# Keys, query weights and output weights of a decode kernel loaded in 4 KB runs, raw keys through the value ring

## The chip, the cores and the metric

One core of one Trainium2 chip. The metric is the device time of one launch in microseconds (us). A time "of n runs" is a median; all runs of this study were in the fast state, with a granted clock of 1.0. In the profiles PE is the matmul engine and PEld its weight loads, DVE the vector engine, ACT the scalar engine, POOL GpSimd, and SPq the queue of SyncE, which issues all loads.

## The reference, cut to what matters

Two rounds of grouped-query attention for one new token, each followed by a small FFN. Both attention rounds read the same key and value cache, 8 sequences x 8 key heads x 8192 positions x 128, in bf16: 134 MB of keys and 134 MB of values.

```python
def _A_ref(x, k_cache, v_cache, wq, wo):          # x [8,1,512], wq [512,4096], wo [4096,512]
    q = (x @ wq).reshape(B, Sq, 32, 128).transpose(0, 2, 1, 3)
    scores = einsum("bhqd,bhkd->bhqk", q, k) * 128 ** -0.5      # four query heads share a key head
    p = softmax(scores); o = einsum("bhqk,bhkd->bhqd", p, v)
    return o.transpose(0, 2, 1, 3).reshape(B, Sq, 4096) @ wo
x = x + _A_ref(layernorm(x), ...);  x = x + _B_ref(layernorm(x), w1, w2)     # _B_ref: w2 @ silu(w1 @ x)
x = x + _A_ref(layernorm(x), ...);  x = x + _B_ref(layernorm(x), w1, w2)
```

The second round's queries depend on the first round's result, so a sequence's values are read twice. Its keys (17 MB) are read once and kept turned on the chip for the second round.

## The kernel before

A "unit" is one round of attention (layer 0 or 1) for one sequence b and key head g. A pass interleaves layer 1 of sequence b with layer 0 of sequence b+1. All loads come in pieces of 512 KB ("granules", 4 KB on each of 128 partitions), in one fixed order on one queue; a load waits for its place, and those behind it wait too. Values, wq and wo go into a ring of 10 places, keys into 33 places of their own, where DVE turns them (32x32 transposes of 32-bit words) into the place before.

```python
N_GRAN = 10; N_PIECE = 33; N_DEF = 2              # ring places, key pieces, units held over a boundary

def load_v(b, g, P):                              # 4 KB contiguous per partition
    return load_gran(f"v{b}.{g}.{P}", v_src(b, g)[P], 1)

def load_k(b, g):
    src = A_k_cache[b, g].rearrange("(p c4 cg) d -> p c4 (cg d)", p=128, c4=4)
    for q in range(4):                            # four runs of 1 KB per partition
        m = 4 * (G * b + g) + q                   # may start when the piece lying there was scored by layer 1
        n = plan.load(f"k{b}.{g}.{q}", 0.5, None, None, [scored.get(m - N_PIECE + 1)])
        ... dma(sp, piece(m + 1)..., src[:, :, 4 * DH * q:4 * DH * (q + 1)], ...)

def load_wq(g): return load_gran(f"wq{g}", wq_v[:, :, R * DH * g:R * DH * (g + 1)], KT)   # 1 KB runs
def load_wo(g): return load_gran(f"wo{g}", wo_v[:, R * g:R * (g + 1), :], R)              # 1 KB runs

def turns(b, g):                                  # two transposes of 512 words per piece
    ... tn.append(plan.add(f"t{b}.{g}.{q}", "DVE", 1.25, turn, count[0] + 0.5, [kn] + tn[-1:]))
# scores of piece q wait for turn q; then maximum (DVE), all-reduce (POOL), subtraction (DVE),
# exponent (ACT), sum (DVE), all-reduce (POOL), reciprocal (DVE)
```

A small planner simulates engines and loads at build time with these durations. The order in which it finds things done becomes the static instruction order of each engine; the semaphores come from the data alone. Between two passes lies the "boundary": layer 0 of the last unit, output projection, FFN, norm, the first query of layer 1, its scores and exponents. Two units of the pass before are held back so that their values can be loaded meanwhile.

## Time and profile before

| | before |
|---|---|
| time, median of 3 | 1325.4 us |
| bytes moved by the load queue | 481.9 MB |
| mean rate over the span | 366 GB/s |
| packets of 1 KB / 4 KB | 206608 / 65536 |
| DVE, PE busy | 54%, 49% |

The prediction below shows the rows for the queue and the rates. These two rows of the page belong beside them: the busy time of each engine, and the shares of the chain that ended last.

```profile
PE 652.5 (49%) x20384; PEld 598.1 (45%) x20384; DVE 721.2 (54%) x1456; ACT 52.2 (4%) x138; POOL 116.3 (9%) x291
DMA 50%; DVE 16%; issue 14%; SPq 14%; PE 4%; POOL 2%; POOLq 0%; ACT 0%; DVEq 0%
```

No engine is near full, and half the last chain is transfers. Three stretches of the windows view, a pass, the first boundary and a later one (columns: start and end, length, busy time of five engines with instruction counts, granted clock, DMA share, GB/s):

```profile
160.00:290.00 130.00, 63.32 (x1950) 57.63 (x1951) 76.05 (x146) 4.99 (x13) 10.98 (x27) 1.00 1.06 380
132.50:160.00 27.50, 14.53 (x468) 13.56 (x468) 13.40 (x32) 1.33 (x4) 3.57 (x8) 1.00 0.68 240
610.00:635.00 25.00, 13.62 (x439) 12.68 (x436) 13.22 (x34) 1.15 (x3) 2.98 (x7) 1.00 0.95 348
```

Within a pass the queue is full at the rate of its mix of 1 and 4 KB; at the boundaries it is not full.

### The profile page before, as it was taken

Reading aid. Unit: us, or ns where it says so; the run is one execution under the profiler, and the core shown is the slowest. Engines: PE = TensorE matmul, PEld = TensorE weight load, DVE = VectorE, ACT = ScalarE, POOL = GpSimd, SP = SyncE. Lnnn points to the kernel's source line nnn. Section 1 sums busy time; section 2 is a strip of 40 time slices with the busy share of each in tenths; the row PEclk is TensorE's granted clock in tenths of the full one; section 3 lists DMA queues with packets and bytes.
Section 4 is the critical chain, followed back from the end, with each engine's and each line's share of the span. In section 5 each row is a group of like instructions: output and inputs, shape, how many; then the busy total and the mean of one; then the engine's idle time right before and its main releaser. Section 6 shows DMA issues by size and latency. Waiting matters only on the chain.

```text
span 1325.2 us, 45128 instructions
## 1 busy us (share of the span) xinstructions
PE 652.5 (49%) x20384; PEld 598.1 (45%) x20384; DVE 721.2 (54%) x1456; ACT 52.2 (4%) x138; POOL 116.3 (9%) x291
## 2 busy tenths in 40 slices
PE   2324544555544554445554454554554555444555
PEld 2323544444544544445444454444543454444554
DVE  7644465735568265673466645484465736567221
ACT  0000000000000000000000000000000000000000
POOL 1000100100000010010000000000000100001000
DMA  9999799999999999999999999999999999999995
GB/s 327 373 369 381 264 380 379 371 391 357 380 377 373 357 383 379 375 377 359 379 385 369 389 350 379 377 373 388 330 385 376 369 378 371 378 378 376 387 367 198
DMA packets 287392, 484.78 MB, mean 366 GB/s; under 512 B 14544, under 2 KB 221152, under 8 KB 287200
## 3 DMA queue, kind: packets, MB, share of 16 engines
q1 hardware_dynamic: 287200, 481.90, 101.3%
q8 instruction: 160, 2.62, 0.8%
q14 instruction: 32, 0.26, 0.1%
HBM read 481.83 MB, written 0.01 MB: 364 GB/s over the span
## 4 chain that ended last, share of the span: by engine, by line
DMA 50%; DVE 16%; issue 14%; SPq 14%; PE 4%; POOL 2%; POOLq 0%; ACT 0%; DVEq 0%
DMA kts<-in_A_k_cache_dram 30%; DVE kts L609 14%; DMA ring<-in_A_v_cache_dram 14%; SPq L310 14%; DMA ring<-in_A_wq_dram 6%; PE ot L733 1%; POOL small L695 1%; PE misc L571 1%; POOL small L676 1%; DVE sc L681 1%; PE misc L479 0%; PE sc L659 0%; DVE small L671 0%; PE yt L761 0%; DVE small L690 0%
## 5 line engine op out<-in xcount | busy, mean ns | idle before, releaser
L609 DVE STREAM_TRANSPOSE kts<-kts 128x512 uint32<-128x512 uint32 x512 | 511.2, 1073 | 71.7 <-DMA kts<-in_A_k_cache_dram 63.4
L659 PE MATMUL sc<-bd,kts 128*128 128x16 bf16 x8192 | 279.5, 175 | 285.0 <-DVE kts L609 214.1
L659 PEld LDWEIGHTS sc<-bd,kts 128*128 128x128 bf16 x8192 | 248.5, 104 | 303.4 <-DVE kts L609 226.8
L733 PE MATMUL ot<-p,ring 128*128 128x4 bf16 x8192 | 284.2, 167 | 171.2 <-DMA ring<-in_A_v_cache_dram 156.0
L733 PEld LDWEIGHTS ot<-p,ring 128*128 128x128 bf16 x8192 | 252.3, 104 | 191.6 <-DMA ring<-in_A_v_cache_dram 175.1
L671 DVE TENSOR_REDUCE small<-sc 128x4 f32<-128x256 f32 x128 | 51.9, 405 | 121.9 <-PE sc L659 121.9
L676 POOL PARTITION_ALL_REDUCE small<-small x128 | 48.2, 376 | 713.2 <-DVE small L671 686.4
L686 ACT ACTIVATE p<-sc 128x256 bf16<-128x256 f32 x128 | 49.2, 384 | 1145.9 <-DVE sc L681 1145.9
L571 PE MATMUL misc<-xn,ring 128*128 128x1 bf16 (+1 forms) x1152 | 42.1, 166 | 92.5 <-DMA ring<-in_A_wq_dram 86.4
L695 POOL PARTITION_ALL_REDUCE small<-small x128 | 55.1, 430 | 345.0 <-DVE small L690 303.3
L571 PEld LDWEIGHTS misc<-xn,ring 128*128 128x128 bf16 x1152 | 36.5, 105 | 97.5 <-DMA ring<-in_A_wq_dram 92.3
L745 DVE TENSOR_TENSOR attna<-ot,small 128x4 bf16<-128x4 f32 x64 | 10.0, 157 | 123.8 <-PE ot L733 123.8
L681 DVE TENSOR_TENSOR sc<-sc,small 128x256 f32<-128x256 f32 x128 | 56.6, 443 | 36.5 <-POOL small L676 36.5
L690 DVE TENSOR_REDUCE small<-p 128x4 f32<-128x256 bf16 x128 | 50.8, 397 | 31.0 <-ACT p L686 31.0
L761 PE MATMUL yt<-attna,ring 128*128 128x1 bf16 x1024 | 36.4, 165 | 34.0 <-DVE attna L745 33.9
L643 DVE TENSOR_TENSOR bd<-qx,mask 128x64 bf16<-128x64 f32 x128 | 27.9, 218 | 45.6 <-PE qx L635 45.1
L761 PEld LDWEIGHTS yt<-attna,ring 128*128 128x128 bf16 x1024 | 32.8, 104 | 37.3 <-issue 37.3
L635 PE MATMUL qx<-qab,sel 128*128 128x4 bf16 x256 | 16.5, 169 | 50.2 <-DVE bd L643 39.3
L699 DVE RECIPROCAL small<-small 128x4 f32<-128x4 f32 x128 | 21.4, 167 | 30.9 <-POOL small L695 30.5
L635 PEld LDWEIGHTS qx<-qab,sel 128*128 128x128 bf16 x256 | 11.9, 106 | 52.7 <-DVE bd L643 41.1
L579 DVE CAST qtb<-misc 128x4 bf16<-128x4 f32 x64 | 9.7, 152 | 38.5 <-PE misc L571 38.3
L635 PE MATMUL qx<-qtb,sel 128*128 128x4 bf16 x256 | 16.7, 170 | 15.8 <-DVE qtb L579 15.8
(55 smaller groups left out, 147.4 us busy)
## 6 DMA issues: line engine op xcount, KB each, us to landing
ring<-in_A_v_cache_dram SPq DMA_DIRECT2D x512, 512.0 KB, 10.3
kts<-in_A_k_cache_dram SPq DMA_DIRECT2D x256, 512.0 KB, 10.2
ring<-in_A_wq_dram SPq DMA_DIRECT2D x72, 512.0 KB, 11.0
ring<-in_A_wo_dram SPq DMA_DIRECT2D x64, 512.0 KB, 10.6
kts<-in_A_wo_dram SPq DMA_DIRECT2D x2, 2048.0 KB, 14.6
w<-in_B_w_dram SPq DMA_DIRECT2D x2, 1792.0 KB, 13.7
ring<-in_A_x_dram SPq DMA_DIRECT2D x1, 8.0 KB
out_dram<-ring SPq DMA_DIRECT2D x1, 8.0 KB
```

Source lines behind the costliest of these rows:

```text
L310: eng.dma_start(out_ap, in_ap).then_inc(counter.sem, 16)
L571: steps.append(lambda h=h, kt=kt: pe.matmul(qp[:, h * nb:(h + 1) * nb], wt[:, kt, h * DH:(h + 1) * DH], xn[:, b0:b0 + nb, kt], start=(kt = ...
L609: op(dve, lambda f=f: dve.transpose(new[:, f], raw[:, f]), reads=[res("kp", (m + 1) % N_PIECE)], writes=[res("kp", m % N_PIECE)], add=(f > 0))
L659: steps.append(lambda cg=cg, fe=fe: pe.matmul(sc[:, 16 * cg:16 * cg + 16], kv[:, cg % 4, fe // 2, fe % 2], bd[:, 16 * fe:16 * fe + 16], st ...
L671: op(dve, lambda: dve.tensor_reduce(mxp[sm], sv.rearrange("p (k h) -> p h k", h=R), AX.X, ALU.max), reads=[res(*scr)], writes=[res("mxp", ...
L676: op(pool, lambda: pool.partition_all_reduce(mxa[sm], mxp[sm], 128, bass.bass_isa.ReduceOp.max), reads=[res("mxp", sm)], writes=[res("mxa" ...
L681: op(dve, lambda: dve.tensor_tensor(v, v, mxa[sm].unsqueeze(1).to_broadcast([128, NCH, R]), ALU.subtract), reads=[res("mxa", sm)], writes= ...
L686: op(act, lambda: act.activation(pt[:, :], sv, ACT.Exp, scale=SM_SCALE), reads=[res(*scr)], writes=[res("p", sm)])
L690: op(dve, lambda: dve.tensor_reduce(ssm[sm], pt[:, :].rearrange("p (k h) -> p h k", h=R), AX.X, ALU.add), reads=[res("p", sm)], writes=[re ...
L695: op(pool, lambda: pool.partition_all_reduce(ssa[sm], ssm[sm], 128, bass.bass_isa.ReduceOp.add), reads=[res("ssm", sm)], writes=[res("ssa" ...
L733: steps.append(lambda cg=cg, k=k: pe.matmul(ot[:, 0:R], vt[:, cg, :], pt[:, k:k + R], start=(P == 0 and cg == 0), stop=(P == 3 and cg == N ...
L761: steps.append(lambda r=r, dt=dt: pe.matmul(YT[:, dt * nb:(dt + 1) * nb], w[:, r, dt * 128:(dt + 1) * 128], src(g * R + r), start=(g == 0 ...
```

## The change

Every big streamed load gets runs of 4 KB; w2 and the output weights of the second round, each loaded once, keep 1 KB. To allow it, raw keys go into the common ring (now 11 places) and are turned into one of 8 fixed slots; wq comes by rows in two halves of four granules; wo comes with four of its rows per partition, which spreads the 128 elements of a head over partitions in another order, so four small selection matmuls and a mask bring the attention result into that order. The cut diff:

```diff
-N_GRAN = 10
-N_PIECE = 33
+N_GRAN = 11
+T_TURN = 1.2
-    kts = sb([128, N_PIECE * PIECE], BF16, "kts")
+    kts = sb([128, G * SLOT], BF16, "kts")
+    sel2 = sb([128, 4, 4, 32], BF16, "sel2")
-    def load_k(b, g): ...                       # 1 KB runs, into kts
+    def load_k(b, g, c4):
+        src = A_k_cache[b, g].rearrange("(p c4 cg) d -> c4 p (cg d)", p=128, c4=4)
+        return load_gran(f"k{b}.{g}.{c4}", src[c4], 1)
-    def load_wq(g): ...
+    def load_wq(half, kt):
+        return load_gran(f"wq{half}.{kt}", wq_v[:, kt, GR * half:GR * (half + 1)], 1)
-        return load_gran(f"wo{g}", wo_v[:, R * g:R * (g + 1), :], R)
+        return load_gran(f"wo{g}", A_wo.rearrange("(g p j) d -> g p (j d)", g=G, j=R)[g], 1)
     # queries(): once per half; 16, then 48 matmuls; the four wq granules are given back after the last
     # turns(): one transpose of 1024 words per granule
+            n = plan.add(f"t{b}.{g}.{c4}", "DVE", T_TURN, turn, count[0] + 0.5, [kn] + scored.get(g, []) + tn[-1:])
+            frees(n, "ring", kn)
     # scores: all four steps wait for the fourth turn (before: step q for turn q)
     # layer 0, per unit:
-            dve.tensor_tensor(attna[:, hd], ot, rcp, mult)
+            act.activation(attna[:, hd], ot, Copy)
+            pe.matmul(ot[:, 8 + R * j:...], sel2[:, j], attna[:, hd])      # j = 0..3
+            dve.tensor_tensor(zt, ot[:, 8:24], rcp * mask, mult)
     # out-projection: 16 matmuls with 4 columns instead of 1, summed over the columns once per sequence
... (cut)
```

More of the change, by code (lines that the diff above doesn't have):

```diff
@@ L245, in _build @@
     GR = SLOT // 4
-    PIECE = SLOT // 4
     NCG = 16
@@ L271, in _build @@
     xn = sb([128, NB, KT], BF16, "xn")
+    ysum = sb([128, KT], FP32, "ysum")
     negm = sb([128, 8], FP32, "negm")
@@ L278, in _build @@
     ps = [sb([128, NCH * R], BF16, f"p{i}") for i in range(N_P + N_DEF)]
-    small = sb([128, N_P + N_DEF, 5, R], FP32, "small")
-    mxp, mxa, ssm, ssa, rcp = ([small[:, i, j, :] for i in range(N_P + N_DEF)] for j in range(5))
+    zts = [sb([128, R * R], BF16, f"z{i}") for i in range(N_OT)]
+    small = sb([128, N_P + N_DEF, 6, R], FP32, "small")
+    mxp, mxa, ssm, ssa, rcp, rcm = ([small[:, i, j, :] for i in range(N_P + N_DEF)] for j in range(6))
     SC = [bank(f"sc{i}") for i in range(N_SC)]
@@ L288, in _build @@
     syn = Sync(nc, ctx)
-    ksem = [DmaCounter(syn.new_sem(f"kp{i}")) for i in range(N_PIECE)]
+    ksem = [DmaCounter(syn.new_sem(f"kt{i}")) for i in range(2)]
     rsem = [DmaCounter(syn.new_sem(f"ring{i}")) for i in range(N_GRAN)]
@@ L327, in gran, with slot @@
         return ring[:, i * GR:(i + 1) * GR]
-    def piece(m, n=1):
-        at = m % N_PIECE
-        assert at + n <= N_PIECE
-        return kts[:, at * PIECE:(at + n) * PIECE]
+    def slot(i, n=1):
+        return kts[:, i * SLOT:(i + n) * SLOT]
     plan = Plan()
@@ L354, in v_src @@
         return A_v_cache[b, g].rearrange("(P n r) d -> P n (r d)", P=4, n=128)
-    def load_k(b, g):
-        src = A_k_cache[b, g].rearrange("(p c4 cg) d -> p c4 (cg d)", p=128, c4=4)
-        ns = []
-        for q in range(4):
-            m = 4 * (G * b + g) + q
-            n = plan.load(f"k{b}.{g}.{q}", 0.5, None, None, [scored.get(m - N_PIECE + 1)])
-            def emit(m=m, q=q):
-                dma(sp, piece(m + 1).rearrange("p (c4 x) -> p c4 x", c4=4),
-                    src[:, :, 4 * DH * q:4 * DH * (q + 1)], ksem[(m + 1) % N_PIECE],
-                    writes=[res("kp", (m + 1) % N_PIECE)])
-            n.emit = emit
-            ns.append(n)
-        return ns
-    def load_wq(g):
-        return load_gran(f"wq{g}", wq_v[:, :, R * DH * g:R * DH * (g + 1)], KT)
+    def load_k(b, g, c4):
[3 more added lines that the diff above has]
+        return load_gran(f"wq{half}.{kt}", wq_v[:, kt, GR * half:GR * (half + 1)], 1)
     def load_wo(g):
-        return load_gran(f"wo{g}", wo_v[:, R * g:R * (g + 1), :], R)
+        return load_gran(f"wo{g}", A_wo.rearrange("(g p j) d -> g p (j d)", g=G, j=R)[g], 1)
     def frees(n, pool, src):
@@ L513, in consts @@
             op(pool, lambda a=a: pool.tensor_copy(sv[:, :, :, a, :], iv), reads=[res("ident")], writes=[res("sel")])
+            op(pool, lambda a=a: pool.tensor_copy(
+                sel2[:, :, a, :], ident[:, :].rearrange("p (dd j) -> p j dd", j=4)),
+                reads=[res("ident")], writes=[res("sel2")])
         op(pool, lambda: pool.memset(expo[:, :], -0.5), writes=[res("expo")])
@@ L558, in _build @@
     x_n.give = N_GRAN - 1
-    last_q = [None]
-    def queries(tag, prio, g, wn, b0, nb, deps):
-        qp = MI[:, 0:R * nb]
-        def mul():
-            wt = gran(wn.give).rearrange("p (kt c) -> p kt c", kt=KT)
-            steps = []
-            for h in range(R):
-                for kt in range(KT):
-                    steps.append(lambda h=h, kt=kt: pe.matmul(
-                        qp[:, h * nb:(h + 1) * nb], wt[:, kt, h * DH:(h + 1) * DH], xn[:, b0:b0 + nb, kt],
-                        start=(kt == 0), stop=(kt == KT - 1)))
-            mms(steps, reads=[res("ring", wn.give), res("xn")], writes=[res("misc")])
-        def copy():
-            hd = slice(R * g, R * g + R)
-            if nb == 1:
-                op(dve, lambda: dve.tensor_copy(qtb[:, hd], qp), reads=[res("misc")], writes=[res("qtb", g)])
-            else:
-                op(dve, lambda: dve.tensor_copy(qab[:, :, hd], qp.rearrange("p (h b) -> p b h", b=nb)),
-                   reads=[res("misc")], writes=[res("qab", g)])
-        m = plan.add(f"{tag}.q{g}", "PE", 0.7, mul, prio, [wn, last_q[0]] + deps)
-        frees(m, "ring", wn)
-        last_q[0] = plan.add(f"{tag}.qc{g}", "DVE", 0.17, copy, prio, [m])
-        return last_q[0]
@@ new lines, in queries, with mul, copy @@
+    def queries(tag, prio, half, b0, nb, deps):
+        wn = [load_wq(half, kt) for kt in range(KT)]
+        out_n = {}
+        last = []
+        for g0, g1 in ((4 * half, 4 * half + 1), (4 * half + 1, 4 * half + 4)):
+            nh = R * (g1 - g0)
+            qp = MI[:, 0:nh * nb]
+            def mul(g0=g0, nh=nh, qp=qp):
+                steps = []
+                for h in range(nh):
+                    c = (R * g0 + h) * DH - GR * half
+                    for kt in range(KT):
+                        steps.append(lambda h=h, kt=kt, c=c: pe.matmul(
+                            qp[:, h * nb:(h + 1) * nb], gran(wn[kt].give)[:, c:c + DH], xn[:, b0:b0 + nb, kt],
+                            start=(kt == 0), stop=(kt == KT - 1)))
+                mms(steps, reads=[res("ring", w.give) for w in wn] + [res("xn")], writes=[res("misc")])
+            def copy(g0=g0, g1=g1, qp=qp):
+                hd = slice(R * g0, R * g1)
+                if nb == 1:
+                    op(dve, lambda: dve.tensor_copy(qtb[:, hd], qp), reads=[res("misc")],
+                       writes=[res("qtb", g) for g in range(g0, g1)])
+                else:
+                    op(dve, lambda: dve.tensor_copy(qab[:, :, hd], qp.rearrange("p (h b) -> p b h", b=nb)),
+                       reads=[res("misc")], writes=[res("qab", g) for g in range(g0, g1)])
+            m = plan.add(f"{tag}.q{g0}", "PE", 0.65 * (g1 - g0), mul, prio, wn + deps + last)
+            last = [plan.add(f"{tag}.qc{g0}", "DVE", 0.17, copy, prio, [m])]
+            for g in range(g0, g1):
+                out_n[g] = last[0]
+        for w in wn:
+            frees(m, "ring", w)
+        return out_n
@@ L600, in turns, with turn @@
     def turns(b, g):
-        m0 = 4 * (G * b + g)
         tn = []
-        for q, kn in enumerate(load_k(b, g)):
-            def turn(m=m0 + q):
-                raw = piece(m + 1).bitcast(U32).rearrange("p (c4 cg f j) -> p f c4 cg j", c4=4, cg=4, f=2)
-                new = piece(m).bitcast(U32).rearrange("p (f cg i c4) -> p f c4 cg i", f=2, cg=4, i=32)
-                for f in range(2):
-                    op(dve, lambda f=f: dve.transpose(new[:, f], raw[:, f]),
-                       reads=[res("kp", (m + 1) % N_PIECE)], writes=[res("kp", m % N_PIECE)], add=(f > 0))
-            tn.append(plan.add(f"t{b}.{g}.{q}", "DVE", 1.25, turn, count[0] + 0.5, [kn] + tn[-1:]))
+        new = slot(g).bitcast(U32).rearrange("p (k i c4) -> p c4 k i", i=32, c4=4)
+        for c4 in range(4):
+            kn = load_k(b, g, c4)
+            def turn(kn=kn, c4=c4):
+                raw = gran(kn.give).bitcast(U32).rearrange("p (k j) -> p k j", j=32)
+                op(dve, lambda: dve.transpose(new[:, c4], raw), reads=[res("ring", kn.give)],
+                   writes=[res("kt", g)], add=(c4 > 0))
+            n = plan.add(f"t{b}.{g}.{c4}", "DVE", T_TURN, turn, count[0] + 0.5, [kn] + scored.get(g, []) + tn[-1:])
+            frees(n, "ring", kn)
+            tn.append(n)
         kept[b, g] = tn
@@ L618, in keys @@
         pr = u
-        m0 = 4 * (G * b + g)
         tn = kept[b, g]
@@ L654, in score @@
             def score(q=q):
-                kv = piece(m0 + q).rearrange("p (f cg n e) -> p cg f e n", f=2, cg=4, e=2)
+                kv = slot(g).rearrange("p (cg f n e) -> p cg f e n", f=2, cg=NCG, e=2)
                 steps = []
@@ L659, in score @@
                         steps.append(lambda cg=cg, fe=fe: pe.matmul(
-                            sc[:, 16 * cg:16 * cg + 16], kv[:, cg % 4, fe // 2, fe % 2],
+                            sc[:, 16 * cg:16 * cg + 16], kv[:, cg, fe // 2, fe % 2],
                             bd[:, 16 * fe:16 * fe + 16], start=(fe == 0), stop=(fe == 3)))
-                mms(steps, reads=[res("kp", (m0 + q) % N_PIECE), res("bd", u % N_BD)], writes=[res(*scr)], add=(q > 0))
+                mms(steps, reads=[res("kt", g), res("bd", u % N_BD)], writes=[res(*scr)], add=(q > 0))
             sn.append(plan.add(f"s{u}.{q}", "PE", 0.75, score, pr - 1,
-                               [tn[q], bn] + ([old[1]] if old else []) + sn[-1:]))
-            if layer == 1:
-                scored[m0 + q] = sn[q]
+                               [tn[3], bn] + ([old[1]] if old else []) + sn[-1:]))
+        if layer == 1:
+            scored[g] = [sn[-1]]
         sv = sc[:, 0:NCH * R]
@@ L699, in rec @@
             op(dve, lambda: dve.reciprocal(rcp[sm], ssa[sm]), reads=[res("ssa", sm)], writes=[res("rcp", sm)])
+            if layer == 0:
+                op(dve, lambda: dve.tensor_tensor(rcm[sm], rcp[sm], mask[:, :], ALU.mult),
+                   reads=[res("rcp", sm), res("mask")], writes=[res("rcm", sm)])
         n1 = plan.add(f"mx{u}", "DVE", 0.42, mx, pr - 1, sn)
@@ L739, in values, with norm, cast, spread @@
             vs.append(n)
-        dst = attna[:, hd] if layer == 0 else qab[:, b, hd]
-        dres = res("attna", g) if layer == 0 else res("attnb", g, b)
-        def norm():
-            op(dve, lambda: dve.tensor_tensor(dst, ot[:, 0:R], rcp[sm], ALU.mult),
-               reads=[res("ot", o), res("rcp", sm)], writes=[dres])
-        h["n"] = plan.add(f"n{u}", "DVE", 0.17, norm, pr - 2, [vs[-1], h["rc"]])
+        if layer == 1:
+            def norm():
+                op(dve, lambda: dve.tensor_tensor(qab[:, b, hd], ot[:, 0:R], rcp[sm], ALU.mult),
+                   reads=[res("ot", o), res("rcp", sm)], writes=[res("attnb", g, b)])
+            h["n"] = plan.add(f"n{u}", "DVE", 0.17, norm, pr - 2, [vs[-1], h["rc"]])
+        else:
+            zt = zts[o]
+            def cast():
+                op(act, lambda: act.activation(attna[:, hd], ot[:, 0:R], ACT.Copy), reads=[res("ot", o)],
+                   writes=[res("attna", g)])
+            def spread():
+                steps = [lambda j=j: pe.matmul(
+                    ot[:, 8 + R * j:8 + R * j + R], sel2[:, j].rearrange("p a k -> p (a k)"), attna[:, hd],
+                    start=True, stop=True) for j in range(R)]
+                mms(steps, reads=[res("sel2"), res("attna", g)], writes=[res("ot", o)])
+            def own():
+                v = ot[:, 8:8 + R * R].rearrange("p (j h) -> p j h", h=R)
+                op(dve, lambda: dve.tensor_tensor(
+                    zt[:, :].rearrange("p (j h) -> p j h", h=R), v,
+                    rcm[sm].unsqueeze(1).to_broadcast([128, R, R]), ALU.mult),
+                    reads=[res("ot", o), res("rcm", sm)], writes=[res("z", o)])
+            n = plan.add(f"cast{u}", "ACT", 0.2, cast, pr - 2, [vs[-1]])
+            n = plan.add(f"spread{u}", "PE", 0.2, spread, pr - 2, [n])
+            h["n"] = plan.add(f"own{u}", "DVE", 0.17, own, pr - 2, [n, h["rc"]])
+            h["z"] = o
@@ L749, in values, with out_proj_a, mul @@
         ot_users.append(h["n"])
         p_users[sm] = [vs[-1], h["n"]]
-    def out_proj(h, wt, wres, src, srcres, nb, deps):
+    def out_proj_a(h, prev):
+        g, wn, o = h["g"], h["wo"], h["z"]
+        zt = zts[o]
+        def mul():
+            w = gran(wn.give).rearrange("p (j d) -> p j d", j=R)
+            steps = []
+            for j in range(R):
+                for dt in range(KT):
+                    steps.append(lambda j=j, dt=dt: pe.matmul(
+                        YT[:, dt * R:(dt + 1) * R], w[:, j, dt * 128:(dt + 1) * 128], zt[:, R * j:R * j + R],
+                        start=(g == 0 and j == 0 and dt == 0), stop=(g == G - 1 and j == R - 1),
+                        skip_group_check=True))
+            mms(steps, reads=[res("ring", wn.give), res("z", o)], writes=[res("yt")], add=g > 0)
+        n = plan.add(f"w{h['u']}", "PE", 0.65, mul, count[0] - 3, [h["n"], wn, prev])
+        frees(n, "ring", wn)
+        return n
@@ L754, in out_proj, with out_proj_b @@
+    def out_proj_b(h, wn, prev):
         g = h["g"]
         def mul():
-            w = wt()
+            w = slot(2 * (g // 4)).rearrange("p (h d) -> p h d", h=16)
             steps = []
@@ L761, in mul @@
                     steps.append(lambda r=r, dt=dt: pe.matmul(
-                        YT[:, dt * nb:(dt + 1) * nb], w[:, r, dt * 128:(dt + 1) * 128], src(g * R + r),
+                        YT[:, dt * NB:(dt + 1) * NB], w[:, R * (g % 4) + r, dt * 128:(dt + 1) * 128],
+                        qab[:, :, R * g + r],
                         start=(g == 0 and r == 0 and dt == 0), stop=(g == G - 1 and r == R - 1),
                         skip_group_check=True))
-            mms(steps, reads=wres() + srcres, writes=[res("yt")], add=g > 0)
-        return plan.add(f"w{h['u']}", "PE", 0.65, mul, count[0] - 3, [h["n"]] + deps)
+            mms(steps, reads=[res("wo_all", g // 4)] + [res("attnb", g, b) for b in range(NB)],
+                writes=[res("yt")], add=g > 0)
+        return plan.add(f"e.w{g}", "PE", 0.65, mul, count[0] - 3, [h["n"], wn, prev])
     free_yt = [None]
@@ L773, in a_values @@
         values(h, wo=h["g"])
-        wn = h["wo"]
-        g = h["g"]
-        y_now[0] = out_proj(
-            h, lambda: gran(wn.give).rearrange("p (h d) -> p h d", h=R), lambda: [res("ring", wn.give)],
-            lambda hh: attna[:, hh:hh + 1], [res("attna", g)], 1, [wn, y_now[0] if g else free_yt[0]])
-        frees(y_now[0], "ring", wn)
+        y_now[0] = out_proj_a(h, y_now[0] if h["g"] else free_yt[0])
     ffn_deps = []
@@ L790, in add @@
         def add():
-            op(dve, lambda: dve.tensor_tensor(xs[:, b, :], YT[:, 0:KT], xs[:, b, :], ALU.add),
-               reads=[res("yt"), res("xs")], writes=[res("xs")])
-        return plan.add(f"c{b}.x2", "DVE", 0.15, add, prio, [y_now[0]])
+            op(dve, lambda: dve.tensor_reduce(
+                ysum[:, :], YT[:, 0:KT * R].rearrange("p (k h) -> p k h", h=R), AX.X, ALU.add),
+                reads=[res("yt")], writes=[res("ysum")])
+            op(dve, lambda: dve.tensor_tensor(xs[:, b, :], ysum[:, :], xs[:, b, :], ALU.add),
+               reads=[res("ysum"), res("xs")], writes=[res("xs")])
+        return plan.add(f"c{b}.x2", "DVE", 0.3, add, prio, [y_now[0]])
     wo_all = []
-    wo_at = [4 * G * (NB - 1) + 4 * g for g in (0, 2)]
     def load_wo_all():
         for i in range(2):
-            n = plan.load(f"woall{i}", 2.0, None, None, [scored[wo_at[i] + q] for q in range(4)])
+            n = plan.load(f"woall{i}", 2.0, None, None, scored[2 * i])
             def emit(i=i):
-                at = wo_at[i] % N_PIECE
-                dma(sp, piece(at, 4).rearrange("p (h d) -> p h d", h=16), wo_v[:, 16 * i:16 * i + 16, :], ksem[at],
-                    writes=[res("kp", at + q) for q in range(4)] + [res("wo_all", i)])
+                dma(sp, slot(2 * i).rearrange("p (h d) -> p h d", h=16), wo_v[:, 16 * i:16 * i + 16, :], ksem[i],
+                    writes=[res("kt", 2 * i), res("wo_all", i)])
             n.emit = emit
@@ L826, in _build @@
     first_q = {}
+    second_q = {}
     for b in range(-1, NB):
@@ L847, in advance @@
                     turns(kb, g)
-                    if kb == 0:
-                        first_q[g] = queries("f", count[0] - 5, g, load_wq(g), 0, NB, [f5])
+                    if kb == 0 and g % 4 == 0:
+                        first_q.update(queries("f", count[0] - 5, g // 4, 0, NB, [f5]))
                     made[k] = keys(0, kb, g, first_q[g])
                 else:
-                    q = queries(f"c{b}", count[0] - 3, g, load_wq(g), b, 1, [ready])
-                    made[k] = keys(1, kb, g, q, held_units.index(k) if k in held_units else None)
+                    if g % 4 == 0:
+                        second_q.update(queries(f"c{b}", count[0] - 3, g // 4, b, 1, [ready]))
+                    made[k] = keys(1, kb, g, second_q[g], held_units.index(k) if k in held_units else None)
         for i, v in enumerate(vs):
@@ L870, in _build @@
     for h in ends[-G:]:
-        g = h["g"]
-        w = out_proj(
-            h, lambda g=g: piece(wo_at[g // 4], 4).rearrange("p (h d) -> p h d", h=16)[:, 4 * (g % 4):4 * (g % 4) + 4],
-            lambda g=g: [res("wo_all", g // 4)], lambda hh: qab[:, :, hh],
-            [res("attnb", g, b) for b in range(NB)], NB, [wo_all[g // 4], w])
+        w = out_proj_b(h, wo_all[h["g"] // 4], w)
     def e_x2():
```

## The prediction

> **What bounds the kernel now.** I read the page from the top: engines, slices, DMA. No engine is busy over 54% (DVE), yet the DMA row stands at 9 from end to end. The queue part says what kind of packets fill it.
>
> ```profile
> DMA  9999799999999999999999999999999999999995
> GB/s 327 373 369 381 264 380 379 371 391 357 380 377 373 357 383 379 375 377 359 379 385 369 389 350 379 377 373 388 330 385 376 369 378 371 378 378 376 387 367 198
> DMA packets 287392, 484.78 MB, mean 366 GB/s; under 512 B 14544, under 2 KB 221152, under 8 KB 287200
> q1 hardware_dynamic: 287200, 481.90, 101.3%
> ```
>
> The queue is full, and still the GB/s row swings between 357 and 391. 221152 - 14544 = 206608 packets lie between 512 B and 2 KB. The code accounts for them as 1 KB runs: keys 256 loads x 512 = 131072, wq 72 x 512 = 36864, wo 64 x 512 = 32768, the late wo 4096, w2 1792, x and the output 16. 287200 - 221152 = 66048 are larger: 512 value loads x 128 = 65536 of 4 KB, and 512 of 3.5 KB for w1. (The 14544 tiny ones are semaphore writes, 16 a load.)
>
> So I asked for stretches in which, by the order of the issues, one kind alone is moved; the last column is GB/s, the one before it the DMA share.
>
> ```profile
> core 0: us, PE busy (x) PEld busy (x) DVE busy (x) ACT busy (x) POOL busy (x), PEclk, DMA share, GB/s
> 27.00:32.00 5.00, 0.98 (x32) 0.83 (x29) 4.22 (x7) 0.38 (x1) 0.49 (x2) 1.00 1.10 349
> 600.00:605.00 5.00, 2.54 (x72) 2.24 (x72) 0.92 (x5) 0.00 (x0) 0.54 (x1) 1.00 1.02 405
> 758.00:763.00 5.00, 3.49 (x113) 3.27 (x114) 1.21 (x6) 0.00 (x0) 0.60 (x1) 1.00 1.04 411
> 1282.00:1287.00 5.00, 4.43 (x160) 4.25 (x157) 1.75 (x8) 0.00 (x0) 0.80 (x2) 1.00 1.10 349
> ```
>
> First row: keys (with some wq), all 1 KB. Last: the late wo, 1 KB at another address pattern. The same 349 both times, so run length sets the rate and not the pattern. The middle rows, values alone: 405 and 411; I take 407. With 16 engines a 4 KB packet costs 16 x 4096 / 407 = 161.0 ns and a 1 KB packet 16 x 1024 / 349 = 46.95 ns; the difference, 114.05 ns for 3 KB, is 38.0 ns per KB, which leaves 8.9 ns for a packet of any size.
>
> Work at these rates: 206608 KB-packets 211.6 MB / 349 = 606 us; values 268.4 MB / 407 = 660; w1 1.8 MB at about 400 = 5. Sum 1271 of the 1325 us span. The other **54 us** are time in which the queue moved little, and I located them by windows of 5 us against these rates: about 5 at the start, 10 at the first layer boundary (132 to 160 us, 240 GB/s), 17 at the six next ones (2 to 4 each), 2 before the last pass, 14 after the last load, 6 scattered.
>
> A boundary in the timeline, first of the issuing queue, then of DVE:
>
> ```profile
> 600.77 2.88 SPq L310 DMA_DIRECT2D ring<-in_A_wq_dram  x2
> 603.74 6.85 SPq L310 DMA_DIRECT2D ring<-in_A_v_cache_dram  x4
> 616.27 1.22 SPq L310 DMA_DIRECT2D kts<-in_A_k_cache_dram  x2
> ```
>
> ```profile
> 617.88 0.23 DVE L643 TENSOR_TENSOR bd<-qx,mask 128x64 bf16<-128x64 f32 x1 [1.33 <-PE qx L635]
> 621.19 1.99 DVE L609 STREAM_TRANSPOSE kts<-kts 128x512 uint32<-128x512 uint32 x2 [3.08 <-DMA kts<-in_A_k_cache_dram]
> 623.03 0.36 DVE L671 TENSOR_REDUCE small<-sc 128x4 f32<-128x256 f32 x1
> ```
>
> From 610.6 to 616.27 nothing is issued: the next load is a key piece, and its place is free only when layer 1 has scored the piece that lies there, which waits for the FFN and norms. So the pipe runs dry; then DVE, in order, sits 3 us on the late key before it can do the maximum of the other unit.
>
> **What the Trainium skill says.** "DMA: Bandwidth & Descriptors", Why small descriptors are slow (HBM only): a fixed overhead of some 3 cycles a packet, 27% at 256 B. The direction agrees; the trace's 8.9 ns also costs 1 KB runs 19% of their 47 ns, so the 512 B given under Specifications there as the minimum for line rate is not enough here. The same page's fabric ceiling of 435 GB/s agrees with my slope (16 KB / 38.0 ns = 431 GB/s). "HBM Reference", Specifications: a core alone measures some 425 GB/s, above its 358 share; agrees, with values at 407. "Vector Engine (DVE) Microarchitecture Reference", 3.8: a transpose sustains one element per cycle per lane. The trace differs:
>
> ```profile
> L609 DVE STREAM_TRANSPOSE kts<-kts 128x512 uint32<-128x512 uint32 x512 | 511.2, 1073 | 71.7 <-DMA kts<-in_A_k_cache_dram 63.4
> ```
>
> 1073 ns for 512 elements of 32 bits is 2.1 ns each, about two of its cycles.
>
> **The change, part by part.**
> 1. *Runs.* Keys, wq and wo become 4 KB runs: 131072 + 36864 + 32768 = 200704 packets become 50176, so 150528 fewer. x 8.9 ns / 16 = **-84 us**. (Check: 205.5 MB x (1/349 - 1/407) = 84.) The late wo and w2 stay at 1 KB. All of this lies on the path, as the queue is the bound. New total work 1271 - 84 = 1187 us.
> 2. *Buffers.* Before: ring of 10 granules and 33 key pieces, the keys turned nearly in place. After: ring of 11, keys land in it, and 8 fixed slots hold the turned ones; same memory. At a boundary, after the eight held value loads, the queue could issue 2 wq + 4 values = 6 granules before it met the blocked key. Now 4 wq + 4 values + 3 keys = 11 fill the ring, since a raw key needs no scored slot. Five granules more at 1.29 us (512 KB / 407 GB/s) = 6.4 us of cover. The chain up to the query gets longer: cast on ACT, four matmuls, a masked product, one more DVE reduce, some 0.8 us by 0.2 us instructions. Net 5.6: first boundary 10 to about 4.5; the six others 17 to about 4; -18 us.
> 3. *DVE.* 512 transposes of 512 become 256 of 1024: 256 x 2.1 = 540 us, unchanged. 64 more small products for the mask and 8 reduces, 0.16 us each: +12 us, beside the loads. A pair of units loads 14 granules, 18 us, and gives DVE 4 x 2.1 + about 3.7 = 12 us, 67%; in the first pass 10 granules (12.9 us) against 10.4 us, 80%. Not a bound.
> 4. *PE.* 64 x 4 selection matmuls, the out-projection with 4 columns for 1 (165 against 170 ns in the page's rows of 1 and 4 to 8 columns): +10 us on an engine at 49%. Nothing on the path.
> 5. *Query weights by halves.* Four granules are held until the last of 64 matmuls, some 8 us, twice a pass. In a ring of 11 that leaves 7 = 9 us of loads: enough, as a load needs some 3 us when nothing is ahead of it (first x load landing at 2.3 us). At the start the first query needs eight granules instead of five, +1 us.
> 6. *End.* 14 us, the same chain.
>
> Sum: 1187 + 6 (start) + 4.5 + 4 + 2 + 14 + 6 = **1223 us**, -7.7%.
>
> **Rivals.** *(a) The ring starves.* Landed keys now sit where values should land: four keys arrive in 5.2 us and take 8.4 to turn, and layer-0 values wait for scores that start only after the fourth turn (before: after each). I count for one unit: last key lands at 0, turned by 6, scored by 8.5, exponent by 11; its values land from 6.5 to 11.6, so four of them wait. 11 - 4 leaves 7 in flight. Against starving: that count, and the median of 10 us from issue to landing, which is queueing and shows how deep the queue stands. For it: the static DVE order in the kernel was planned with 1.2 us a turn, not 2.1. If it costs 0.5 to 1 us in each of 64 key units, 32 to 64 us come back: 1255 to 1287. *(b) The boundaries do not gain*, because the chain there is bound elsewhere: 1241. *(c) Long runs help less where rows lie apart* (keys 16 KB, wq 8 KB between partitions, values adjacent): at 390 GB/s for them, 205.5 MB cost 22 us more: 1245. Against: keys and wo had the same 349. *(d) No stall but start and end*: 1187 + 20 = 1207, the floor.
>
> **Range and chances.** The 84 us rest on rates that the windows repeat to 1%, so they are the sure part; the 18 us of the boundaries and the ring are the unsure one. 1207 is the floor, (b) and (c) near the top: 1207 to 1247. Two per cent is 1299; only a starving worse than (a) gets there: faster 0.96, same 0.03, slower 0.01.
>
> **What would show it.** Packets under 2 KB fall to about 20500 and the total to about 136700; pair stretches rise from 380 to 400 or more; windows at the boundaries rise from 340 to near 400 with key issues before the first scores; a transpose takes 2.1 us; DVE and PE keep their busy times. Wrong would be: a GB/s row under 395 in the middle of a pass, with the issuing queue waiting on DVE transposes (rival a), or all at 9 in the DMA row and under 400 (rival c).

## The result, and the profile after

1245.7 us (median of 4, 1242.6 to 1247.1) against 1325.8: the ratio is 0.9395, 95% interval 0.9375 to 0.9415, so 6% faster. (Ratios here are the mean time of one kernel's runs over that of the other's of the same rounds, so not quite the ratio of the medians.) The forecast was 1223 with a range of 1207 to 1247: inside, but 23 us above the forecast. The page's rows that answer to those of before:

```profile
PE 631.6 (51%) x20640; PEld 593.0 (48%) x20640; DVE 708.4 (57%) x1236; ACT 63.0 (5%) x202; POOL 117.0 (9%) x295
DMA  9999999999999999999999999999999999999995
GB/s 362 407 398 408 337 371 408 408 408 356 393 408 408 407 371 407 407 408 399 376 409 407 407 394 373 408 408 408 371 389 408 407 407 364 410 407 408 394 339 208
DMA packets 136865, 484.80 MB, mean 389 GB/s; under 512 B 14544, under 2 KB 20448, under 8 KB 136672
q1 hardware_dynamic: 136672, 481.90, 98.7%
L605 DVE STREAM_TRANSPOSE kts<-ring 128x1024 uint32<-128x1024 uint32 x256 | 503.2, 1988 | 116.6 <-DMA ring<-in_A_k_cache_dram 116.4
```

Read the GB/s row first: 407 to 410 in half the slices, where before it swung between 357 and 391; that is the rate I took for 4 KB runs. Packets are as forecast to the piece (20448 under 2 KB, 136672 in the queue). But every fourth or fifth slice or so is a dip to between 337 and 376. Those are the boundaries. In windows, a pass first, then pieces of the first boundary, then of a later one:

```profile
170.00:270.00 100.00, 49.97 (x1616) 46.75 (x1617) 63.26 (x102) 5.42 (x18) 9.38 (x23) 1.00 1.03 408
130.00:135.00 5.00, 4.18 (x143) 4.05 (x144) 1.04 (x6) 0.00 (x0) 0.00 (x0) 1.00 0.40 128
157.50:165.00 7.50, 4.47 (x155) 4.31 (x156) 6.33 (x8) 0.17 (x1) 0.84 (x2) 1.00 0.81 281
882.50:890.00 7.50, 4.83 (x148) 4.43 (x148) 7.50 (x14) 0.77 (x2) 1.24 (x3) 1.00 0.84 285
902.50:907.50 5.00, 2.06 (x71) 1.89 (x69) 4.37 (x5) 0.17 (x1) 0.00 (x0) 1.00 0.95 318
```

There are two dips per boundary: one just after the chain has yielded its first exponents (882 to 890), in which DVE is busy all 7.50 of 7.50 us, and a second some 15 us later. The first boundary has one more before them, at 130 to 135, when the chain has not yet yielded. There the ring is full, as in the forecast's count, and the queue waits 10.9 us for a place that holds wq:

```profile
SPq L89 <- PE misc L563: 10.9, 1, 10.9
```

To put a number on all dips I use the trace's packet records: **transfer** is the number of packets times the forecast's two rates, 161.0 ns for 4 KB and 46.95 ns for 1 KB, over 16 engines, with some 5 us for w1; **stall** is the span less that.

| | span | transfer | stall |
|---|---|---|---|
| before | 1325.2 | 1270.5 | 54.7 |
| after | 1245.3 | 1186.4 | 59.0 |
| forecast of after | 1223 | 1187 | 36 |

The transfer column is counted and not measured: it agrees with the forecast because the packets do. What tests the two rates is a pass. There 14 granules, of which 6 had 1 KB runs before, should move at 380 GB/s before and 407 after; the windows show 380 and 408. The stall, which I had expected to shrink by 18 us, grew by 4. It now belongs to other waits. The issuing queue's waits, longest first (who it waited for: us in all, times, longest), and below them the one of the kernel before that answers to the first:

```profile
SPq L89 <- DVE kts L605: 270.6, 146, 8.2
SPq L89 <- PE ot L733: 252.9, 246, 4.8
SPq L89 <- PE misc L563: 96.4, 17, 10.9
```

```profile
SPq L310 <- DVE kts L609: 41.6, 45, 3.6
```

Most of these waits are mere flow control with loads still in flight. But waits for turns grew from 41.6 to 270.6 us: places in the ring now come back when DVE has turned a key. The same queue at a later boundary (start, length, what, how many):

```profile
860.30 5.43 SPq L312 DMA_DIRECT2D ring<-in_A_v_cache_dram  x4
867.61 7.63 SPq L312 DMA_DIRECT2D ring<-in_A_k_cache_dram  x4
875.30 11.53 SPq L312 DMA_DIRECT2D ring<-in_A_v_cache_dram  x7
886.92 0.38 SPq L312 DMA_DIRECT2D ring<-in_A_wo_dram  x1
```

The first key is issued at 867.61, well before the first query at 874.7. So the dry spell shown in the forecast, when no key could be issued before layer 1 had scored, is gone at this boundary, and the windows of 2.5 us stay at 403 GB/s or more up to 875. What follows is new: seven value loads take until 886.8. The longest wait of the queue between 850 and 883, 5.2 us, is for a turn.

Two places in DVE's timeline show why. After the chain of this boundary:

```profile
880.93 2.00 DVE L605 STREAM_TRANSPOSE kts<-ring 128x1024 uint32<-128x1024 uint32 x1
882.78 0.48 DVE L678 TENSOR_TENSOR sc<-sc,small 128x256 f32<-128x256 f32 x1
```

The subtraction at 882.78, on which the exponents and so the values of the first unit wait, was ready 1.2 us earlier (POOL ended its all-reduce at 881.55) but stands behind a turn. And some 15 us behind the first boundary:

```profile
145.89 0.16 DVE L743 TENSOR_TENSOR qab<-ot,small 128x4 bf16<-128x4 f32 x1
153.42 1.98 DVE L605 STREAM_TRANSPOSE kts<-ring 128x1024 uint32<-128x1024 uint32 x1 [7.37 <-DMA ring<-in_A_k_cache_dram]
155.25 0.69 DVE L668 TENSOR_REDUCE small<-sc 128x4 f32<-128x256 f32 x2
```

DVE waits 7.37 us for the second unit's first key, which is late, and behind it in DVE's order stand the maxima of two units whose scores PE had finished by 150. Their values lie in the ring meanwhile, and the ring is full at 157: the second dip.

### The profile page after: what moved, and what is told of

Read it like the earlier page. It is cut to its first block, busy times and chain, and to the rows that moved or that the text cites. A ratio compares the mean times of both kernels' runs of the same rounds, so it can differ in the third digit from the quotient of the medians.

```text
span 1245.3 us, 45478 instructions
## 1 busy us (share of the span) xinstructions
PE 631.6 (51%) x20640; PEld 593.0 (48%) x20640; DVE 708.4 (57%) x1236; ACT 63.0 (5%) x202; POOL 117.0 (9%) x295
## 2 busy tenths in 40 slices
DMA packets 136865, 484.80 MB, mean 389 GB/s; under 512 B 14544, under 2 KB 20448, under 8 KB 136672
## 3 DMA queue, kind: packets, MB, share of 16 engines
q1 hardware_dynamic: 136672, 481.90, 98.7%
## 4 chain that ended last, share of the span: by engine, by line
DMA 41%; DVE 25%; issue 20%; PE 10%; SPq 2%; POOL 2%; ACT 0%; POOLq 0%; DVEq 0%
DMA ring<-in_A_k_cache_dram 24%; DVE kts L605 19%; DMA ring<-in_A_v_cache_dram 10%; DMA ring<-in_A_wq_dram 7%; PE sc L656 5%; PE ot L733 2%; SPq L312 2%; DVE sc L678 2%; DVE small L668 2%; PE misc L563 1%; POOL small L673 1%; DVE small L687 1%; POOL small L692 1%; DVE bd L640 0%; PE yt L784 0%
## 5 line engine op out<-in xcount | busy, mean ns | idle before, releaser
L605 DVE STREAM_TRANSPOSE kts<-ring 128x1024 uint32<-128x1024 uint32 x256 | 503.2, 1988 | 116.6 <-DMA ring<-in_A_k_cache_dram 116.4
L733 PE MATMUL ot<-p,ring 128*128 128x4 bf16 x8192 | 287.4, 167 | 177.0 <-DMA ring<-in_A_v_cache_dram 115.7
L733 PEld LDWEIGHTS ot<-p,ring 128*128 128x128 bf16 x8192 | 255.5, 104 | 193.6 <-DMA ring<-in_A_v_cache_dram 131.1
L784 PE MATMUL yt<-z,ring 128*128 128x4 bf16 x1024 | 36.8, 166 | 93.1 <-DVE z L762 89.8
L784 PEld LDWEIGHTS yt<-z,ring 128*128 128x128 bf16 x1024 | 33.0, 104 | 96.2 <-issue 96.0
L563 PE MATMUL misc<-xn,ring 128*128 128x1 bf16 (+1 forms) x1152 | 36.2, 166 | 68.7 <-DMA ring<-in_A_wq_dram 62.1
L563 PEld LDWEIGHTS misc<-xn,ring 128*128 128x128 bf16 x1152 | 33.8, 104 | 71.1 <-issue 64.9
L571 DVE CAST qtb<-misc 128x4 bf16<-128x4 f32 (+1 forms) x32 | 5.3, 166 | 54.3 <-PE misc L563 54.3
L743 DVE TENSOR_TENSOR qab<-ot,small 128x4 bf16<-128x4 f32 x64 | 10.0, 157 | 43.6 <-PE ot L733 43.4
L762 DVE TENSOR_TENSOR z<-ot,small 128x16 bf16<-128x16 f32 x64 | 10.5, 164 | 37.7 <-PE ot L755 37.7
```

The costliest lines, as they stand in the source:

```text
L563: steps.append(lambda h=h, kt=kt, c=c: pe.matmul(qp[:, h * nb:(h + 1) * nb], gran(wn[kt].give)[:, c:c + DH], xn[:, b0:b0 + nb, kt], start= ...
L605: op(dve, lambda: dve.transpose(new[:, c4], raw), reads=[res("ring", kn.give)], writes=[res("kt", g)], add=(c4 > 0))
L733: steps.append(lambda cg=cg, k=k: pe.matmul(ot[:, 0:R], vt[:, cg, :], pt[:, k:k + R], start=(P == 0 and cg == 0), stop=(P == 3 and cg == N ...
L784: steps.append(lambda j=j, dt=dt: pe.matmul(YT[:, dt * R:(dt + 1) * R], w[:, j, dt * 128:(dt + 1) * 128], zt[:, R * j:R * j + R], start=(g ...
```

## The experiments

**Theory.** The missing gain is the ring at the boundaries. Four granules of wq, four raw keys and values fill it; after the chain the places come back only at the pace of DVE, in an order that was planned with too short a turn. **Rivals.** (R1) The ring's size or cover alone decides. (R2) DVE's order alone decides. (R3) The held wq granules. (R4) Long runs help less for keys. Each run below that was built was correct and timed in rounds against the kernel before. "Slower" and "won" are differences of medians from different rounds, in which the kernel before itself moved between 1323.1 and 1325.8 us; by the ratios they come out up to 2 us otherwise.

**1. Plan with the measured turn** (`T_TURN = 1.2` to `2.05`).

> The changed kernel, whose static order of DVE work was planned with 1.2 us a transpose, planned with 2.05 us (the profile shows 1.99). Nothing else differs. If the stalls at the layer boundaries (34 us in all, of which I had expected 10) come from transposes that stand in the DVE order ahead of the maximum and subtraction of another unit (DVE sat 7.4 us on a late key at 146 us), a better planned order should win a good part back: 1228 to 1238 us. If the ring's size alone decides, nothing: 1243 to 1248. It may also be worse, if the order only gets different: up to 1255.

Measured 1265.8 us (ratio 0.9554, 0.9537 to 0.9571): 20 us slower than the change. The true duration makes a worse order here; the stall grew to 78 us, with new dips in mid-pass (near the second half of wq). So order matters much, which speaks against R1 alone, but my guess at which order is good was wrong.

**2. A third held unit** (`N_DEF = 2` to `3`).

> The changed kernel with three held units at a boundary instead of two: four more value loads (4 x 1.29 = 5.2 us of cover) that need nothing from the chain of FFN, norms and queries. If a boundary stalls because the ring of 11 is full before the chain yields, each of the seven later boundaries wins up to its stall of 3 to 5 us: 1222 to 1232 us. The first boundary has no held units and keeps its 7.7 us. If the stalls come from the order of DVE after the chain, the time stays within 1240 to 1247.

Measured 1241.9 us (0.9376, 0.9359 to 0.9392), 4 us won where R1 asked for 14 to 24, and the intervals of the two ratios overlap. The profile shows why. At the boundary that the change shows at 882, which comes some 7 us earlier here, the first dip is nearly gone (393 GB/s and more from 862.5 to 892.5), the second is not:

```profile
885.92 0.42 DVE L668 TENSOR_REDUCE small<-sc 128x4 f32<-128x256 f32 x1 [2.40 <-PE sc L656]
890.42 1.98 DVE L605 STREAM_TRANSPOSE kts<-ring 128x1024 uint32<-128x1024 uint32 x1 [4.07 <-DMA ring<-in_A_k_cache_dram]
892.54 0.42 DVE L678 TENSOR_TENSOR sc<-sc,small 128x256 f32<-128x256 f32 x1
```

```profile
892.50:897.50 5.00, 3.43 (x113) 3.26 (x114) 4.90 (x12) 0.77 (x2) 1.23 (x3) 1.00 0.79 306
```

The maximum at 885.92 needs its subtraction about 0.9 us later, and gets it at 892.54, behind a turn whose key landed at 890.42. The load rate falls to 306 GB/s right after, as the values that wait for those exponents fill the ring.

**3. One ring place less** (`N_GRAN = 11` to `10`).

> The changed kernel with a ring of 10 granules instead of 11. If the ring's size sets the stalls, a granule is 1.29 us of cover: at two stalls per pass and eight boundaries at least 8 x 1.29 = 10 and up to 20 us slower, 1255 to 1266 us, and the loss sits at the boundaries. If the ring is not the bound there, 1243 to 1249.

Measured 1258.9 us (0.9503, 0.9477 to 0.953): 13 us slower, stall 74. A place is worth what the theory said. (Twelve places do not fit: by the message of run 12 this kernel has some 1 KB a partition left, and a place takes 4 KB.)

**4. Query weights per group in 1 KB runs again.**

```diff
-    def load_wq(half, kt):
-        return load_gran(f"wq{half}.{kt}", wq_v[:, kt, GR * half:GR * (half + 1)], 1)
+    def load_wq(g):
+        return load_gran(f"wq{g}", wq_v[:, :, R * DH * g:R * DH * (g + 1)], KT)
     # and queries() as in the kernel before: 16 matmuls a group, its granule freed after them
```

> The changed kernel with the query weights loaded per group in 1 KB runs again, as before the change: 27648 packets more, 27648 x 8.9 ns / 16 = +15 us by rate. But a granule of wq is given back after 16 matmuls and not four together after 64. If the four held granules cause the boundary stalls, those shrink by 5.2 us or less per boundary and the sum is about 1230 to 1245; if they do not matter, 1258 to 1263.

Measured 1249.1 us (0.9429, 0.9411 to 0.9448), between the two expectations: transfer 1201.8 (+15.4), stall 47.6 (-11.4). Runs of 4 KB for wq win only some 3 us net, and the two intervals still touch. The stall that went is not proved to be the four held granules', because run 6 shows that slower transfers alone, though of far more packets, take about as much away. At the first boundary (125 to 152.5 us) it did not go: 6.2 us here, 5.7 in the change.

**5. Turns behind the subtraction, for every key unit from the second pass on** (planner only).

```diff
-    [kn] + scored.get(g, []) + tn[-1:])
+    [kn] + scored.get(g, []) + tn[-1:] + (last_sub if b and not c4 else []))
     # last_sub: the subtraction of the unit before, of either layer
```

> The changed kernel with one more dependency in its planner (no semaphore, order only): from the second pass on, the first transpose of a key unit is put behind the score subtraction of the unit before it, so that DVE does not sit in front of a key that has not landed while a finished maximum waits. In the changed kernel this sat 7.4 us at 146 us and 3.0 us at 894 us. If that head-of-line wait makes the second stall of each boundary (about 1.5 to 3 us each, 8 of them) and the first turn before the first subtraction part of the first, this wins 8 to 18 us: 1228 to 1238. If the ring is full whatever the order, 1242 to 1249.

Measured 1258.4 us (0.9499, 0.9483 to 0.9515): 13 us slower, stall 70. A miss. At the boundary the first unit's four raw keys now wait until 889 for their turn, so the ring stays full from both sides: the rate falls to 220 to 230 GB/s from 887.5 to 892.5. R2 in this blunt form falls.

**6. Keys in 1 KB runs, through the same ring.**

```diff
-    src = A_k_cache[b, g].rearrange("(p c4 cg) d -> c4 p (cg d)", p=128, c4=4)
-    return load_gran(f"k{b}.{g}.{c4}", src[c4], 1)
+    src = A_k_cache[b, g].rearrange("(p c4 cg) d -> p c4 (cg d)", p=128, c4=4)
+    return load_gran(f"k{b}.{g}.{c4}", src[:, :, 4 * DH * c4:4 * DH * (c4 + 1)], 4)
```

> The changed kernel, keys through the same ring but in four 1 KB runs per partition again; wq and wo stay at 4 KB. 98304 packets more at 8.9 ns over 16 engines is +55 us of transfer. With the stalls unchanged 1300 us; since a granule now takes 1.5 us of wire, the ring covers longer and up to 10 us of stall may go: 1288 to 1302. If long runs of keys did not pay because their rows lie 16 KB apart, it would be near 1265.

Measured 1291.4 us (0.9757, 0.9741 to 0.9772): 46 us slower than the change; transfer 1241.3 (+54.9), stall 48.3 (-10.7). R4 falls: most of the gain is the keys. And it shows how the two terms trade: when granules come more slowly, the queue waits less for turns (134.6 us against 270.6) and stalls shrink.

**7, 8. Runs 5 and 2 together, then with run 4.**

> Both together: the order of e5_ordsub and a third held unit. If the held unit won only 4 us alone because the second stall behind the boundary stayed, the two add up to more than their sum: 1220 to 1232. If e5_ordsub does nothing, 1238 to 1243.

> Order, third held unit, and query weights per group in 1 KB runs. Transfer +15 us against e7_ordsub_def3. The query weights per group alone cost only 3 us net, so they took some 12 us of stall away; if e7_ordsub_def3 has taken away the same stalls, this is 8 to 15 us slower than it; if different ones, within 3 us of it.

Measured 1249.0 us (0.9433, 0.9416 to 0.945) and 1261.2 (0.9522, 0.9505 to 0.9539). The first is worse than run 2 by 7: the blunt order costs with a third held unit too. The second is 12 us slower than the first, within the range for "the same stalls", though with the blunt order in both this says little.

**9. Output weights in 1 KB runs, without selection matmuls.** (The layer-0 normalisation and projection as in the kernel before.)

> The changed kernel with the per-unit output weights in 1 KB runs again and with them the plain normalisation and out-projection (no cast, no selection matmuls, no masked product). 24576 packets more at 8.9 ns over 16 engines: +14 us. The chain to the FFN loses the 0.8 us I put on it, eight times, -6 us if all of it is on the path. If only the rate counts, 1259; if the longer chain took part of the gain, 1251 to 1256.

Measured 1256.5 us (0.9483, 0.9462 to 0.9504): 11 us slower; transfer +13.7, stall 58.1 (-0.9) in the profiled run, which was the slowest of the four. By the medians the stall shrinks by 3 us. So the longer chain costs 1 to 3 us in all, not the six I had thought possible, and part of that may be the trade seen in run 6.

**10. A third held unit, and the order for the second key unit of a pass alone.**

```diff
-N_DEF = 2
+N_DEF = 3
-    [kn] + scored.get(g, []) + tn[-1:])
+    [kn] + scored.get(g, []) + tn[-1:] + (last_sub if b and g == 1 and not c4 else []))
     # last_sub: the subtraction of the layer-0 unit before
```

> The changed kernel with three held units, and the planner's extra order for the second key unit of a pass alone: its first transpose comes behind the score subtraction of the first. The first key unit stays as it was, since putting it last in e5_ordsub only kept four raw keys longer in a full ring. If the second stall of a boundary is the wait of DVE before that one transpose (4.07 us at 886 us in e2_def3), about 2 us at seven boundaries: 1226 to 1236. If the granules are short anyway, 1238 to 1246.

Measured 1235.7 us (0.9326, 0.931 to 0.9342), in the range of "this one transpose".

**11. Three layer-1 units lead a pass, three held.** (`ks = two[:2]` to `two[:3]`, later ones shifted by one.)

> Three held units, and the order of units changed: three layer-1 units instead of two lead a pass, so that their values are loaded before the first keys and DVE has no transposes between the chain and the first exponents. If the stall comes from raw keys that hold ring places and DVE just when the chain yields, the first stall of the boundaries shrinks by 2 to 4 us, also at the first boundary, which has no held unit: 1218 to 1232. If values only take the places that keys held, 1236 to 1246.

Measured 1247.6 us (0.9417, 0.9399 to 0.9434), 6 us slower than run 2 and above both expectations: values took the places that the keys had held, and the keys came later.

**12. Four held units.** It was not built: the memory lacked 192 bytes a partition. No result.

> The version of e10_ord1_def3 with four held units. The boundaries that still stall in it lose about 1 to 2 us before the first exponents; 5.2 us more of cover should take that: 1226 to 1233 us. If the third unit already covers what cover can, 1233 to 1239. The first boundary, without held units, and the end stay.

**13. The order of run 10 alone, two held units, 5 rounds.** The best simple version.

> The changed kernel, two held units as it has, with the order of e10_ord1_def3 alone. If the second stall behind each boundary (1.3 to 2.2 us in the changed kernel, more with its slower run-up) is the wait of DVE before the second key unit's first transpose, and does not depend on the cover, about 6 to 12 us: 1234 to 1240. If the order only helps once a third held unit covers the first stall, 1241 to 1246.

Measured 1236.0 us (5 runs, 1234.1 to 1237.9; 0.9337, 0.9325 to 0.935): 10 us faster than the change (8 by the ratios), with one planner rule and no other instruction. The interval lies clear of the change's 0.9375 to 0.9415. Stall 47.9. DVE behind the first boundary, to be laid beside the three lines of the kernel after:

```profile
149.84 0.43 DVE L679 TENSOR_TENSOR sc<-sc,small 128x256 f32<-128x256 f32 x1
150.32 0.42 DVE L679 TENSOR_TENSOR sc<-sc,small 128x256 f32<-128x256 f32 x1
152.43 1.98 DVE L606 STREAM_TRANSPOSE kts<-ring 128x1024 uint32<-128x1024 uint32 x1 [0.55 <-DMA ring<-in_A_k_cache_dram]
```

Both subtractions now come at 150, not behind a turn at 153, and the wait for the key has shrunk from 7.37 to 0.55 us. The same stretch of both kernels, first the change:

```profile
150.00:165.00 15.00, 4.79 (x159) 4.57 (x160) 10.38 (x16) 0.91 (x3) 1.56 (x4) 1.00 0.92 342
150.00:165.00 15.00, 7.36 (x246) 6.98 (x247) 9.78 (x15) 0.94 (x3) 1.10 (x3) 1.00 1.01 395
```

Between 146 and 165 the issuing queue waited 8.2 us for turns in the change, and not at all here. The boundary that the change shows at 882 comes some 9 us earlier and shows what the rule leaves. The first dip is still there, with DVE busy 8.58 of 10 us; in place of the second the rate is 407:

```profile
870.00:880.00 10.00, 6.67 (x236) 6.43 (x233) 8.58 (x15) 0.77 (x2) 1.63 (x4) 1.00 0.88 331
885.00:905.00 20.00, 9.03 (x298) 8.51 (x299) 12.24 (x22) 1.71 (x5) 2.61 (x7) 1.00 1.02 407
```

The planner moved other instructions with it: some 190 of DVE's 1236 stand in another order than in the change. That the gain is the rule's own is read from where it lies, in the table below.

With the third held unit (run 10) the stall is 47.7, the same. So what the unit won alone in run 2, if it won anything, is among what the order wins.

## Why the prediction was right or wrong, point by point

The stall by place, in us, summed in the same way over stretches of the traces (the forecast's terms beside it):

| | before | after | forecast of after | run 13 |
|---|---|---|---|---|
| start, 20 us | 3.1 | 3.5 | 6 | 3.6 |
| first boundary | 10.4 | 8.6 | 4.5 | 7.6 |
| six next boundaries | 17.7 | 23.8 | 4 | 13.0 |
| boundary before the last pass | 1.8 | 5.0 | 2 | 5.3 |
| end | 17.0 | 15.4 | 14 | 15.4 |
| elsewhere | 4.9 | 3.0 | 6 | 3.1 |

- **The bound and the runs: right.** The queue was the bound, and a pass went from 380 to 408 GB/s, as the two rates say. With them only 3.0 us of stall are left outside boundaries, start and end. That 150528 packets fewer take 84 us off the transfer is a count at these rates, and so is what undoing one part puts back: 54.9 (keys), 15.4 (wq) and 13.7 us (wo). In time the three cost 46, 3 and 11 us, 60 together, as the stalls shrank each time.
- **The buffers: the step that failed.** "Net 5.6: first boundary 10 to about 4.5; the six others 17 to about 4; -18 us." At the later boundary shown the cover came as counted: keys are issued before the query, and the pipe stays full until the chain has yielded. At the first boundary it ran out before: 128 GB/s from 130 to 135. The "some 8 us" for which wq was to be held fail there: its four granules were issued by 111.8, and the queue waited for a place of theirs until about 132.5. Above all I counted how long the ring lasts and not how it is emptied. The six others, forecast at 4 us, went from 17.7 to 23.8. Stall over the whole run went from 54.7 to 59.0 us. Of the 23 us above my 36, 11 (59.0 to 47.9) are shown by run 13 to be one static order, and they lie at those six boundaries (23.8 to 13.0): DVE sits before a key that has not landed (7.37 us behind the first boundary, 2.97 us up to 896.89 behind the one at 882) while finished maxima and subtractions stand behind it, and their values hold the ring.
- **The other 12 us: only narrowed down.** Run 13 still has 9 us more than forecast at the six boundaries, 3 each at the first and at the last, and less than forecast at the start and elsewhere. The ring's places matter (run 3, 13 us a place). At the first dip DVE is busy without a gap, with four turns of 2 us among the softmax steps. Putting the turns last (run 5) or the keys later (run 11) makes it worse. A third held unit shrinks this dip at the boundary shown in run 2, but no run takes this part off the total. R3, the held wq granules, stays open at the later boundaries.
- **"Not a bound" for DVE: right on average (57%), wrong at the boundaries**, where it was busy for 7.50 of 7.50 us. The average over a pair of units hid it. A transpose of 1024 words takes 1988 ns, forecast 2.1 us. DVE's busy time fell by 13 us and PE's by 21, where I had added 12 and 10.
- **Rival (a), the ring starves: true in kind, wrong in place.** I put it in the 64 key units in mid-pass; passes run at 405 to 408, and it happens only behind boundaries. Of the sign I named for it, one half is there, the issuing queue waiting on transposes (270.6 us against 41.6), and the other is not, under 395 GB/s in the middle of a pass. **Rival (b)**, boundaries gain nothing, 1241, was the nearest in kind, but its reason, a chain that is bound elsewhere, is not what run 13 shows. **Rival (c)** had the nearest number, 1245, by luck: at its 390 GB/s for keys, wq and wo a pass would move at some 400 (6 of 14 granules at 390, the rest at 407), and it moves at 408.
- **The longer chain:** 0.8 us a boundary was allowed; run 9 puts 1 to 3 us on the whole kernel.

## What to carry to other kernels

Where a queue is full, ask first how many packets it moves: rates from two pure stretches of the profile gave the rate of a whole pass within 1% (407 forecast, 408 measured). When a change puts more kinds of data into one ring, count what empties it as well as what fills it, and look at the in-order engine that empties it in the microseconds behind a long dependency and not on average. An instruction that waits for a transfer should not stand in front of ready work in a static order; here one rule of planning was worth 8 to 10 us, while the same rule for every key unit cost 13.

## What the Trainium skill lacked or had wrong

- "DMA: Bandwidth & Descriptors", Specifications: at least 512 B is given as the transfer for line rate. Here 1 KB runs moved 349 GB/s and 4 KB runs 405 to 411. It has no table of this chip's load rate by run length; the two rates here fit 8.9 ns a packet and 38.0 ns a KB on each of 16 engines.
- The same page, "Issuing engines are not separate DMA queues", says of the issue only that it is usually small beside the transfer. Here the issue of a key load took at least 539 ns with 512 runs (before and run 6) and at least 327 ns with 128; wq, also with 512 runs, took at least 378 before. The transfer of such a load is 1.29 to 1.5 us at the rates above. (The medians for keys, 1610 before, 695 in run 6 and 328 after, may hold waits for room in the queue.)
- "Vector Engine (DVE) Microarchitecture Reference", 3.8: one element per cycle and lane for a transpose. 32-bit transposes took 1073 ns for 512 words and 1988 for 1024, which is 1.8 ns for each further word. Products on the same engine took 157 ns at 4 elements a partition and 217 at 64, 1.0 ns for each further element.
